# The opening of a layered kernel reordered: V projection by rows of Wv, two centred first tiles, evacuation per token tile

## The chip, the cores and the metric

The kernel runs on one core of one Trainium2 chip. The metric is device time in microseconds (us), the median of repeated executions. On one core the runs of one kernel mostly agree within 0.1%. Profiles are single executions taken by the hardware profiler; their spans are about 2 us shorter than the run times. Engines are named PE (matmuls), ACT (ScalarE), DVE (VectorE), POOL and SP. In the profiles PEld is PE's weight load, and an SPq line is the time SP spends on issuing a DMA, not the time until its data land. SP computes nothing; here it issues all DMAs, one after the other. PSUM is the memory that PE writes its sums to; an evacuation copies them out of it.

## The reference

```
x = A_x                                          # 2048 tokens x 1024, bf16
x = x + A(layernorm(x))                          # attention in a dilated window of 8, 32 heads of 32
x = x + B(layernorm(x))                          # token-mixing MLP 2048 -> 3584 -> 2048, gelu
x = x + A(layernorm(x))                          # the same weights again
x = x + B(layernorm(x))
# A: qkv = x @ wqkv (1024 x 3072); ...; o @ wo
```

The change concerns only the start of the first A: layernorm of the 16 token tiles (128 tokens each) and V = layernorm(x) @ Wv. Right after it the products for q and k begin, with weights of their own.

## The kernel before

`start_up` builds one list of steps for each engine. Each list is strictly kept in order. For each token tile k: statistics (`S_`, `A_`) on DVE, 1/std (`R_`: an Ln and an Exp) on ACT, the normalisation (`N_`) on DVE, and a transposed copy in `hT`, which is the matmul's stationary operand. Tiles 0 to 4 are transposed on PE (`tr`) and copied out of PSUM by ACT (`C_`); tiles 5 to 15 by a transposing DMA (`T_`). Then 16 matmuls (`V_`) and the evacuation of their sums (`E_`, ACT).

```python
wm = m_tile()
for _ in range(14):                               # warm-up matmuls on zeros
    chain_("PE", lambda: nc.tensor.matmul(wm[:], lhsT=warm[:, 0:P], rhs=warm[:], start=True, stop=True))
...
act = [(R_, 0), (C_, 0, 0), (R_, 1), (C_, 0, 1), (C_, 1, 0), (C_, 1, 1), (R_, 2), (E_, 0, 0), ...
       (R_, 5), (E_, 1, 1), (R_, 6), (E_, 2, 1), (C_, 4, 0), (C_, 4, 1)]
es = [(E_, k, n) for k in range(3, NT) for n in range(NDC)]   # NT = 16, NDC = 2 halves of a tile
rs = [(R_, k) for k in range(7, NT)]
for j, e in enumerate(es):
    act.append(e)
    if rs and j % 4 != 3:                         # three rsqrts per four half-tile evacuations
        act.append(rs.pop(0))
...
dve.append((zero_fill,))                          # after the last norm
dve.append((cast_biases,))
sp = [(T_, k) for k in range(np_, NT)] + [(load_biases,)]     # np_ = 5
...
# in the layer loop
start_up(v, wv)
wts = [None, None]
chain_("SP", load_qk, 0, wts)                     # weights of the first q and k, last on SP
...
for part, n in chunks:                            # part 0 is q, part 1 is k
    in_order(qk_chunk, 0, wts, part, n)           # first q matmuls, L352
```

The weights of q and k are issued on SP after every transposing DMA and after the biases, and the transposing DMAs wait for the norms, which wait for the rsqrts on ACT.

The softmax here doesn't subtract the row's maximum and nothing guards it: scores larger than these inputs give would overflow.

## Time and profile before

| | before |
|---|---|
| median of 6 runs | 1294.20 us (1293.59 to 1294.54) |
| span of the profiled run | 1291.8 us |
| first V matmul starts | 7.80 us |
| last norm ends, last transposing DMA issued | about 42.1 us |
| weights of q and k issued | 47.43 us |
| first q matmul (L352) starts | 65.62 us |

The first lines below are from the profile page (busy us, share of the span, number of instructions; then the chain that ended last, by engine).

```profile
PE 1275.1 (99%) x8286; PEld 593.4 (46%) x8442; DVE 417.1 (32%) x852; ACT 372.8 (29%) x628; POOL 2.4 (0%) x15
...
PE 98%; issue 1%; DVE 0%; ACT 0%
```

PE is the bound, and only time in which it stands idle, or runs slowly, can be won or lost. Next, PE's timeline in the opening: start, duration in us, engine, line, operation, output and inputs, number of matmuls merged, and in brackets the idle time before and what ended it.

```profile
1.38 5.30 PE L268 MATMUL m<-warm 128*128 128x512 bf16 x14 [1.38 <-DVE warm L207]
6.52 0.61 PE L244 MATMUL s<-ident,x 128*128 128x128 bf16 x8
7.80 1.04 PE L255 MATMUL m<-wv,hT 128*128 128x512 bf16 x4 [0.68 <-ACT hT L249]
8.81 0.62 PE L244 MATMUL s<-ident,x 128*128 128x128 bf16 x8
9.40 1.89 PE L255 MATMUL m<-wv,hT 128*128 128x512 bf16 x8
11.61 0.62 PE L244 MATMUL s<-ident,x 128*128 128x128 bf16 x8 [0.32 <-DVE x L188]
```

From the transposes at 6.52 on PE loses only about 1.5 us, in small gaps until 12.28 (an estimate: 59.1 us pass until q begins, and 256 matmuls at 0.216 us with five groups of transposes at 0.45 need 57.5). The last group is the same kernel's timeline (all engines) where the norms of the tiles end, and where q begins.

```profile
41.26 0.20 ACT L175 ACTIVATE rs<-ln 128x1 f32<-128x1 f32 x1
41.50 0.55 DVE L188 TENSOR_SCALAR x<-x,mv,rs 128x1024 bf16<-128x1024 bf16 x1 [0.60 <-ACT rs L175]
...
43.36 0.58 SPq L141 DMA_DIRECT2D b_bf<-in_B_b_dram  x1
...
44.00 3.39 SPq L142 DMA_DIRECT2D b_bf<-in_B_b_dram  x1
...
47.43 1.21 SPq L344 DMA_DIRECT2D wqk<-in_A_wqkv_dram  x2
...
65.62 7.07 PE L352 MATMUL m<-hT,wqk 128*128 128x512 bf16 x32
```

The weights were issued at 47.43 and landed 5.4 us later (median of the two loads), some 13 us before PE asked for them.

### The profile page before, as it was taken

What the parts mean: (1) busy time and instruction counts of PE and PEld (TensorE: products, weight loads), DVE (VectorE), ACT (ScalarE), POOL (GpSimd) and SP (SyncE); (2) the same over time, 40 slices, a digit from 0 to 9 for tenths busy, and PEclk for the clock granted to TensorE, in tenths of its full rate; (3) what the DMA queues carried; (4) which work ended last, traced back from release to release, by engine and by line L of the source; (5) the groups of instructions that cost most, each with busy time, mean ns of one, the idle gap of its engine ahead of it and who ended that gap; (6) DMA issues with size and microseconds to landing.
All of it is one profiled execution on the core that took longest, in us unless ns stands there. A gap on an engine that the chain in (4) does not pass through costs nothing.

```text
span 1291.8 us, 19417 instructions
## 1 busy us (share of the span) xinstructions
PE 1275.1 (99%) x8286; PEld 593.4 (46%) x8442; DVE 417.1 (32%) x852; ACT 372.8 (29%) x628; POOL 2.4 (0%) x15
## 2 busy tenths in 40 slices
PE   9999999999999999999999999999999999999999
PEld 4444444444444444444444444444444444444444
DVE  7457777820000022322300667778100000111111
ACT  5456664431111110000023666644311111000000
POOL 0000000000000000000000000000000000000000
PEclk9999999999999999999999999999999999999999
DMA  8411123742222235466410111247423222334330
GB/s 236 82 46 47 51 82 120 212 139 82 65 82 76 57 110 139 131 154 142 130 33 1 47 50 51 79 151 214 120 65 89 75 60 81 103 106 136 117 92 33
DMA packets 201862, 125.54 MB, mean 97 GB/s; under 512 B 39984, under 2 KB 183600, under 8 KB 201776
## 3 DMA queue, kind: packets, MB, share of 16 engines
q1 hardware_dynamic: 201776, 124.30, 34.2%
q8 instruction: 66, 1.08, 0.4%
q14 instruction: 20, 0.16, 0.0%
HBM read 96.48 MB, written 16.78 MB: 88 GB/s over the span
## 4 chain that ended last, share of the span: by engine, by line
PE 98%; issue 1%; DVE 0%; ACT 0%
PE m L352 17%; PE s L594 15%; PE s L547 15%; PE m L467 8%; PE acc L547 7%; PE m L547 7%; PE acc L594 7%; PE m L594 7%; PE m L337 4%; PE m L255 4%; PE s L383 2%; PE acc L418 1%; PE acc L422 1%; PE m L268 0%; PE s L244 0%
## 5 line engine op out<-in xcount | busy, mean ns | idle before, releaser
L594 PEld LDWEIGHTS <-w 128*128 128x128 bf16 x1820 | 177.0, 98 | 210.2
L547 PEld LDWEIGHTS <-w 128*128 128x128 bf16 x1792 | 175.3, 98 | 211.4
L352 PE MATMUL m<-hT,wqk 128*128 128x512 bf16 x963 | 223.3, 379 | 6.2 <-issue 4.6
L547 PE MATMUL s<-h,w 128*128 128x512 bf16 x878 | 201.2, 379 | 0.8
L594 PE MATMUL s<-g,w 128*128 128x512 bf16 (+1 forms) x912 | 201.0, 374 | 0.7
L596 DVE SCALAR_TENSOR_TENSOR xo<-s,b_sb,xs 128x512 bf16<-128x512 f32 (+1 forms) x33 | 24.4, 739 | 532.9 <-PE s L594 530.8
L352 PEld LDWEIGHTS <-wqk 128*128 128x128 bf16 x1024 | 95.3, 98 | 117.9 <-issue 10.7
L398 DVE TENSOR_TENSOR Pm<-pc,band 32x640 bf16<-32x640 bf16 x256 | 123.5, 483 | 56.3 <-ACT pc L386 49.4
L467 PE MATMUL m<-wo,oT 128*128 128x512 bf16 x500 | 110.6, 379 | 0.8 <-issue 0.3
L547 PE MATMUL acc<-h,w 128*128 128x512 bf16 x440 | 103.1, 379 | 0.5
L594 PE MATMUL acc<-g,w 128*128 128x512 bf16 x436 | 99.7, 379 | 0.5
L547 PE MATMUL m<-h,w 128*128 128x512 bf16 x438 | 98.5, 379 | 0.5
L594 PE MATMUL m<-g,w 128*128 128x512 bf16 (+1 forms) x436 | 96.9, 376 | 0.6
L174 ACT ACTIVATE ln<-mv,eps 128x1 f32<-128x1 f32 x64 | 18.9, 295 | 221.1 <-DVE mv L182 184.9
L467 PEld LDWEIGHTS <-oT 128*128 128x128 bf16 x512 | 49.6, 98 | 60.3 <-issue 1.3
L554 ACT ACTIVATE g<-s,b_sb 128x1024 bf16<-128x1024 f32 x28 | 31.2, 1114 | 158.2 <-PE s L547 146.4
L363 DVE COPY qB<-qs 32x512 bf16<-32x512 bf16 x136 | 38.1, 280 | 99.2 <-ACT qs L359 97.1
L255 PE MATMUL m<-wv,hT 128*128 128x512 bf16 x250 | 55.6, 379 | 1.0 <-ACT hT L249 0.7
L337 PE MATMUL m<-wv,hT 128*128 128x512 bf16 x251 | 55.2, 379 | 0.3
L386 ACT ACTIVATE pc<-s,shift 128x640 bf16<-128x640 f32 x64 | 51.2, 800 | 11.7 <-PE s L383 11.7
L359 ACT CAST qs<-m 128x512 bf16<-128x512 f32 x64 | 37.5, 586 | 48.7 <-PE m L352 47.6
L356 ACT CAST kT<-m 128x512 bf16<-128x512 f32 x64 | 37.5, 586 | 46.4 <-PE m L352 46.4
(58 smaller groups left out, 671.8 us busy)
## 6 DMA issues: line engine op xcount, KB each, us to landing
w<-in_B_w_dram SPq DMA_DIRECT2D x56, 512.0 KB, 3.8
w<-in_B_w_dram SPq DMA_DIRECT2D x64, 448.0 KB, 4.7
wqk<-in_A_wqkv_dram SPq DMA_DIRECT2D x16, 512.0 KB, 5.2
xa<-xn SPq DMA_DIRECT2D x32, 256.0 KB, 2.3
xs<-xa SPq DMA_DIRECT2D x32, 256.0 KB, 3.0
wv<-in_A_wqkv_dram SPq DMA_DIRECT2D x8, 512.0 KB, 5.6
wo<-in_A_wo_dram SPq DMA_DIRECT2D x8, 512.0 KB, 6.4
xr<-in_A_x_dram SPq DMA_DIRECT2D x16, 256.0 KB, 3.4
```

Of the source, the lines that this page charges most:

```text
L255: r = nc.tensor.matmul(pss_[k, n][:], lhsT=hT[:, kt, cols(*order[k])], rhs=wv[n][kt // 4][:, kt % 4, :], start=(kt == 0), stop=(kt == KD - 1))
L337: nc.tensor.matmul(ps[:], lhsT=hT[:, kt, cols(c, i)], rhs=wv[n][kt // 4][:, kt % 4, :], start=(kt == 0), stop=(kt == KD - 1))
L352: mm = nc.tensor.matmul(ps[:], lhsT=wts[part][:, kt, (g % 2) * P:(g % 2 + 1) * P], rhs=hT[:, kt, lo:lo + 512], start=(kt == 0), stop=(kt = ...
L356: nc.scalar.copy(out=kT[u % 2][:, ls], in_=ps[:])
L359: nc.scalar.copy(out=qs[:], in_=ps[:])
L363: nc.vector.tensor_copy(out=qB[u % 2][hp, h, ls], in_=qs[hp, :])
L386: nc.scalar.activation(out=pc[:].rearrange("p (n t) h k -> p n (t h k)", n=2), in_=ss[:, :, 0:2 * HG * GW], func=ACT.Exp, scale=scale, bia ...
L398: mm = nc.vector.tensor_tensor(out=Pm[rp, :, s0:s0 + HB, r * KG:r * KG + GW].rearrange("p h t k -> p t h k"), in0=pc[rp], in1=mk, op=ALU.mult)
L467: mm = nc.tensor.matmul(ps[:], lhsT=oT[g][:, cols(c, i)], rhs=wo[n][g // 4][:, g % 4, :], start=(g == 0), stop=(g == NG - 1))
L547: nc.tensor.matmul(pairs[fl][0][dc], lhsT=wt[c][:, i, fl * P:(fl + 1) * P], rhs=h2[c][i][:, dc * 512:(dc + 1) * 512], start=(k == 0), stop ...
L554: nc.scalar.activation(out=g[fb][:, fl, :].rearrange("p (n d) -> p n d", n=2), in_=t[:], func=ACT.Gelu_apprx_tanh, bias=b1_sb[:, ft:ft + 1])
L594: nc.tensor.matmul(ap, lhsT=w2t[ft // HF][:, ft % HF, c::DIL], rhs=g[ft // GF][:, ft % GF, lo:lo + w], start=(ft == 0), stop=(ft == FT - 1))
```

## The change

Its intent is to start the V product sooner. It has five parts:

1. Tiles 0 and 1 are only centred before their transposes (`M_` on DVE, half of tile 0 on ACT by `Ma`). 1/std is applied when V leaves PSUM. Their `hT` must be rewritten for q and k, so two norms are added on DVE (after those of tiles 8 and 9) and two transposing DMAs at the end of SP's list of transposes.
2. Wv is loaded by rows (all 1024 columns of one block of 128 rows, eight loads), and tiles 0 and 1 take turns row by row.
3. Sums lie in two-bank tiles, three in rotation; transposes move to the small PSUM tiles.
4. One evacuation per token tile (128x1024), not two halves.
5. The rsqrts are placed anew on ACT: one after each evacuation. Warm-up matmuls: 9, plus one after the first transposes, in place of 14. ACT's table load moves into `start_up`.

The core of the diff (cut: the new helper functions, the dependency table, the layout of Wv in the second layer):

```diff
-        for _ in range(14):
-            chain_("PE", lambda: nc.tensor.matmul(wm[:], ...))
+        for _ in range(9):
+            chain_("PE", W_, 1)
...
+        pe = [(tr, 0), (W_, 1), *VV(0, 0), (tr, 1), *VV(0, 1, 2), *VV(1, 0, 1, 2)]
...
+        act = [(Ma, 0, halves[1]), (C_, 0, 0), (C_, 0, 1), (C_, 1, 0), (C_, 1, 1), (R_, 0), (R_, 1), (R_, 2), (C_, 2, 0), (C_, 2, 1),
+               (R_, 3), (E_, 0), (E_, 1), (C_, 3, 0), (C_, 3, 1), (R_, 4), (E_, 2), (C_, 4, 0), (C_, 4, 1), (R_, 5), (E_, 3), (R_, 6)]
+        for k in range(4, NT):
+            act.append((E_, k))
+            if k + 3 < NT:
+                act.append((R_, k + 3))
-        for j, e in enumerate(es):
-            act.append(e)
-            if rs and j % 4 != 3:
-                act.append(rs.pop(0))
...
+            if k in (8, 9):
+                dve.append((N_, k - 8, whole))
-        sp = [(T_, k) for k in range(np_, NT)] + [(load_biases,)]
+        sp = [(T_, k) for k in (*range(np_, NT), 0, 1)] + [(load_biases,)]
```

More of the change, by code (lines that the diff above doesn't have):

```diff
@@ L113, in ln_exp_table @@
         return tc.keep_in_program_order(nc.scalar.preload_act_table_set("natural_log_exp_and_others"))
-    ln_exp_table()
     ident = const.tile([P, P], BF16, name="ident")
@@ L133 @@
                                 pattern=[[-1, GW]], channel_multiplier=1)
+    mv01 = const.tile([P, 2, 2], FP32, name="mv01")
+    rs01 = const.tile([P, 2], FP32, name="rs01")
+    nm0 = const.tile([P, 1], FP32, name="nm0")
     b1_bf = const.tile([P, FT], BF16, name="b1_bf")
@@ L187, in norm_dve @@
     def norm_dve(dst, x, mean, rs):
-        return nc.vector.tensor_scalar(out=dst, in0=x, scalar1=mean, scalar2=rs[:], op0=ALU.subtract, op1=ALU.mult)
+        return nc.vector.tensor_scalar(out=dst, in0=x, scalar1=mean, scalar2=rs, op0=ALU.subtract, op1=ALU.mult)
     def norm_act(dst, x, mean, rs):
@@ L205, in start_up @@
         np_ = 5
+        xc = [x2(f"xc{k}") for k in range(2)]
         warm = x2("warm", [P, 512])
@@ L217, in x_load, with w_load @@
             return r
-        def w_load(n, hf):
-            return nc.sync.dma_start(out=wv[n][hf][:], in_=wq_v[:, hf * (KD // 2):(hf + 1) * (KD // 2),
-                                                                2 * D + n * 512:2 * D + (n + 1) * 512])
+        def w_load(kt):
+            return nc.sync.dma_start(out=wv[kt // 2][:, kt % 2, :], in_=wq_v[:, kt, 2 * D:3 * D])
         def S_(k, cc):
@@ L228, in A_, with B_, M_, Ma @@
         def A_(k):
-            mvs[k] = st("mv", [P, 2])
-            return nc.vector.bn_aggr(out=mvs[k][:], in_=sts[k][:])
+            mvs[k] = mv01[:, k, :] if k < 2 else st("mv", [P, 2])[:]
+            return nc.vector.bn_aggr(out=mvs[k], in_=sts[k][:])
+        def B_(k):
+            return nc.vector.tensor_scalar(out=nm0[:], in0=mvs[k][:, 0:1], scalar1=-1.0, scalar2=None, op0=ALU.mult)
+        def M_(k, h):
+            return nc.vector.tensor_scalar(out=xc[k][:, h], in0=xs[k][:, h], scalar1=mvs[k][:, 0:1], scalar2=None,
+                                           op0=ALU.subtract)
+        def Ma(k, h):
+            return nc.scalar.activation(out=xc[k][:, h], in_=xs[k][:, h], func=ACT.Identity, bias=nm0[:])
         def R_(k):
-            rss[k] = st("rs", [P, 1])
-            return rsqrt(rss[k][:], mvs[k][:, 1:2], 1.0, eps1)
+            rss[k] = rs01[:, k:k + 1] if k < 2 else st("rs", [P, 1])[:]
+            return rsqrt(rss[k], mvs[k][:, 1:2], 1.0, eps1)
         def N_(k, hs):
@@ L241, in tr @@
         def tr(k):
-            tps[k] = pss.tile([P, KD, P], BF16, name="s", tag="s")
+            tps[k] = psm.tile([P, KD, P], BF16, name="m", tag="m")
             for kt in range(KD):
-                r = nc.tensor.transpose(tps[k][:, kt, :], xs[k][:, kt * P:(kt + 1) * P], ident[:])
+                r = nc.tensor.transpose(tps[k][:, kt, :], (xc[k] if k < 2 else xs[k])[:, kt * P:(kt + 1) * P], ident[:])
             return r
@@ L251, in V_, with E_ @@
         def V_(k, n, kts):
-            if kts[0] == 0:
-                pss_[k, n] = m_tile()
+            if k not in pss_:
+                pss_[k] = a_tile() if k % 3 == 1 else s_tile()
             for kt in kts:
-                r = nc.tensor.matmul(pss_[k, n][:], lhsT=hT[:, kt, cols(*order[k])], rhs=wv[n][kt // 4][:, kt % 4, :],
+                r = nc.tensor.matmul(pss_[k][:, n, :], lhsT=hT[:, kt, cols(*order[k])], rhs=wv[kt // 2][:, kt % 2, n * 512:(n + 1) * 512],
                                      start=(kt == 0), stop=(kt == KD - 1))
             return r
-        def E_(k, n):
+        def E_(k):
             c, i = order[k]
-            return nc.scalar.copy(out=v[c][i][:, n * 512:(n + 1) * 512], in_=pss_[k, n][:])
+            dst, src = v[c][i][:].rearrange("p (n d) -> p n d", n=NDC), pss_[k][:]
+            if k < 2:
+                return nc.scalar.activation(out=dst, in_=src, func=ACT.Identity, scale=rss[k])
+            return nc.scalar.copy(out=dst, in_=src)
         def T_(k):
@@ L266, in start_up, with W_ @@
         wm = m_tile()
-        for _ in range(14):
-            chain_("PE", lambda: nc.tensor.matmul(wm[:], lhsT=warm[:, 0:P], rhs=warm[:], start=True, stop=True))
+        def W_(n):
+            for _ in range(n):
+                r = nc.tensor.matmul(wm[:], lhsT=warm[:, 0:P], rhs=warm[:], start=True, stop=True)
+            return r
+        for _ in range(9):
+            chain_("PE", W_, 1)
         halves = (slice(0, D // 2), slice(D // 2, D))
         whole = (slice(0, D),)
+        chain_("ACT", ln_exp_table)
@@ L272, in start_up @@
         chain_("SP", x_load, 0, halves)
         chain_("SP", x_load, 1)
-        chain_("SP", w_load, 0, 0)
+        for kt in range(4):
+            chain_("SP", w_load, kt)
         chain_("SP", x_load, 2)
-        chain_("SP", w_load, 0, 1)
+        chain_("SP", w_load, 4)
+        chain_("SP", w_load, 5)
         chain_("SP", x_load, 3)
-        chain_("SP", w_load, 1, 0)
-        chain_("SP", w_load, 1, 1)
+        chain_("SP", w_load, 6)
+        chain_("SP", w_load, 7)
         for k in range(4, NT):
@@ L281, in start_up, with VV @@
             chain_("SP", x_load, k)
-        lo4, hi4 = range(KD // 2), range(KD // 2, KD)
+        def VV(k, *kts):
+            return [(V_, k, n, [kt]) for kt in kts for n in range(NDC)]
         a8 = range(KD)
-        pe = [(tr, 0), (V_, 0, 0, lo4), (tr, 1), (V_, 0, 0, hi4), (V_, 1, 0, lo4), (tr, 2), (V_, 1, 0, hi4),
-              (V_, 2, 0, a8), (V_, 0, 1, a8), (tr, 3), (V_, 1, 1, a8), (V_, 2, 1, a8), (tr, 4)]
+        pe = [(tr, 0), (W_, 1), *VV(0, 0), (tr, 1), *VV(0, 1, 2), *VV(1, 0, 1, 2)]
@@ L287, in start_up @@
+        for kt in range(3, 6):
+            pe += [*VV(0, kt), *VV(1, kt)]
+        pe += [(tr, 2), *VV(0, 6, 7), *VV(1, 6, 7), (V_, 2, 0, a8), (tr, 3), (V_, 2, 1, a8), (tr, 4)]
         pe += [(V_, k, n, a8) for k in range(3, NT) for n in range(NDC)]
-        act = [(R_, 0), (C_, 0, 0), (R_, 1), (C_, 0, 1), (C_, 1, 0), (C_, 1, 1), (R_, 2), (E_, 0, 0), (C_, 2, 0), (C_, 2, 1),
-               (E_, 1, 0), (R_, 3), (E_, 2, 0), (R_, 4), (E_, 0, 1), (C_, 3, 0), (C_, 3, 1), (R_, 5), (E_, 1, 1), (R_, 6),
-               (E_, 2, 1), (C_, 4, 0), (C_, 4, 1)]
@@ L291, in start_up @@
-        es = [(E_, k, n) for k in range(3, NT) for n in range(NDC)]
-        rs = [(R_, k) for k in range(7, NT)]
-        for j, e in enumerate(es):
-            act.append(e)
-            if rs and j % 4 != 3:
-                act.append(rs.pop(0))
-        dve = [(S_, 0, 0), (S_, 0, 1), (A_, 0), (S_, 1, 0), (N_, 0, halves), (S_, 1, 1), (A_, 1), (N_, 1, whole),
+        act = [(Ma, 0, halves[1]), (C_, 0, 0), (C_, 0, 1), (C_, 1, 0), (C_, 1, 1), (R_, 0), (R_, 1), (R_, 2), (C_, 2, 0), (C_, 2, 1),
+               (R_, 3), (E_, 0), (E_, 1), (C_, 3, 0), (C_, 3, 1), (R_, 4), (E_, 2), (C_, 4, 0), (C_, 4, 1), (R_, 5), (E_, 3), (R_, 6)]
@@ L298, in start_up @@
+        for k in range(4, NT):
+            act.append((E_, k))
+            if k + 3 < NT:
+                act.append((R_, k + 3))
+        dve = [(S_, 0, 0), (S_, 0, 1), (A_, 0), (B_, 0), (M_, 0, halves[0]), (S_, 1, 0), (S_, 1, 1), (A_, 1), (M_, 1, whole[0]),
                (S_, 2, 0), (S_, 2, 1), (A_, 2)]
@@ L300, in start_up @@
             nx = k + 1 < NT
-            if nx:
-                dve.append((S_, k + 1, 0))
-            dve.append((N_, k, whole))
+            if k == 2:
+                dve += [(N_, k, whole), (S_, k + 1, 0)]
+            else:
+                if nx:
+                    dve.append((S_, k + 1, 0))
+                dve.append((N_, k, whole))
             if nx:
                 dve += [(S_, k + 1, 1), (A_, k + 1)]
+            if k in (8, 9):
+                dve.append((N_, k - 8, whole))
         dve.append((zero_fill,))
         dve.append((cast_biases,))
-        sp = [(T_, k) for k in range(np_, NT)] + [(load_biases,)]
+        sp = [(T_, k) for k in (*range(np_, NT), 0, 1)] + [(load_biases,)]
         qs = {"PE": pe, "ACT": act, "DVE": dve, "SP": sp}
-        need = {cast_biases: lambda: (load_biases,) in done, R_: lambda k: k in mvs, N_: lambda k, h: k in rss, tr: lambda k: (N_, k) in done, C_: lambda k, hf: k in tps,
-                V_: lambda k, n, kts: ((C_, k, 1 if kts[-1] == KD - 1 else 0) in done or (T_, k) in done), E_: lambda k, n: (V_, k, n) in done,
-                T_: lambda k: (N_, k) in done}
+        need = {cast_biases: lambda: (load_biases,) in done, R_: lambda k: k in mvs, N_: lambda k, h: k in rss, tr: lambda k: (N_, k) in done if k > 1 else (M_, k) in done and (k == 1 or (Ma, k) in done),
+                B_: lambda k: k in mvs, M_: lambda k, h: k in mvs, Ma: lambda k, h: (B_, k) in done, C_: lambda k, hf: k in tps,
+                V_: lambda k, n, kts: ((C_, k, kts[-1] * 2 // KD) in done or (T_, k) in done), E_: lambda k: (V_, k, 1) in done and (k > 1 or k in rss),
+                T_: lambda k: (N_, k) in done and (k > 1 or (E_, k) in done)}
         done = set()
@@ L325, in load_wv, with fill_wv @@
     def load_wv():
-        return [[wt_("wv", [P, KD // 2, 512]) for _ in range(2)] for _ in range(NDC)]
-    def fill_wv(wv, n):
-        for hf in range(2):
-            nc.sync.dma_start(out=wv[n][hf][:],
-                              in_=wq_v[:, hf * (KD // 2):(hf + 1) * (KD // 2), 2 * D + n * 512:2 * D + (n + 1) * 512])
+        return [wt_("wv", [P, 2, D]) for _ in range(KD // 2)]
+    def fill_wv(wv):
+        for j in range(KD // 2):
+            nc.sync.dma_start(out=wv[j][:], in_=wq_v[:, 2 * j:2 * j + 2, 2 * D:3 * D])
     def v_proj(v, c, i, wv, ns):
@@ L336, in v_proj @@
             for kt in range(KD):
-                nc.tensor.matmul(ps[:], lhsT=hT[:, kt, cols(c, i)], rhs=wv[n][kt // 4][:, kt % 4, :],
+                nc.tensor.matmul(ps[:], lhsT=hT[:, kt, cols(c, i)], rhs=wv[kt // 2][:, kt % 2, n * 512:(n + 1) * 512],
                                  start=(kt == 0), stop=(kt == KD - 1))
@@ L603, in gemm2 @@
             mean, rs = stats(xo, 1.0, eps1)
-            norm_dve(xs[:], xo[:], mean, rs)
+            norm_dve(xs[:], xo[:], mean, rs[:])
             nc.sync.dma_start_transpose(out=hT[:, :, cols(c, i)], in_=xs[:])
@@ L619 @@
         else:
-            fill_wv(wv, 0)
-            fill_wv(wv, 1)
+            fill_wv(wv)
             wts = [None, None]
```

## The prediction

> **What bounds the kernel.** PE is busy 99% of a 1291.8 us span (busy table); the chain that ended last is 98% PE. Only idle PE time can be won. In the opening (timeline, chain of waits, 0 to 66 us) warm-up matmuls run 1.38 to 6.68, transposes start at 6.52, the first V matmul at 7.80 (after the rsqrt, the normalisation, 8 transposes and a copy), with gaps until 12.28. From there V runs at 0.216 us a matmul; the first q matmul (L352) starts at 65.62. V plus transposes need about 57.5 us, so the opening holds about 1.5 us of gaps after 6.5, and the lead before.
>
> **What the change does at the front.** Tiles 0 and 1 are only centred before the transposes; 1/std is applied at the evacuation. That takes Ln 0.29 + Exp 0.20 off the path, but adds a negated mean (a 128x1 DVE operation of this kind takes 0.205 us, group of L493) and puts half of the centring on ACT (estimate 0.7 us, from the 128x512 Gelu's 0.68). Mean is ready at 4.75; I expect ACT's half done at 5.7, transposes done near 6.25, first V matmul near 6.9 (0.9 earlier) (rows of Wv land in time, by the bytes moved per stretch plus the 1.1 us lag that x1 and x4 show). One new stall: R4 sits behind the copies of tile 3 on ACT, so transpose 4 waits about 0.7 us. Net at the front: V ends 0.3 to 1.1 us earlier, about 65.0.
>
> **What it moves at the back.** The order of instructions shows more. Before, ACT's rsqrts ran ahead (three per four half-tile evacuations), so the last norm ended near 42, the last transposing DMA issued at 42.1, biases at 43.4 and 44.0 (issue 3.39 us), wqk at 47.4, landing 5.4 us later at 52.8. Now ACT alternates strictly: whole-tile evacuation k, then rsqrt k+3. Evacuation k waits for V of tile k, so rsqrt 15 follows the evacuation of tile 12. Counting from the start s of V tile 13 on PE: evacuation to s+1.3 (1.11 us as the 128x1024 Gelu), rsqrt to s+1.86, norm (0.55) to s+2.45, last DMA transpose issued s+2.5. Two more transposing DMAs (tiles 0 and 1, 1.24 us of SP each) now stand before the biases. Before, from that issue to the landing of q's weights took 10.7 us; so now s+2.5+10.7+2.5 = s+15.7. V ends at s+10.35. PE therefore waits some 5.3 us for q's weights, however early V started. Earlier transposes still land 1.3 us before PE needs them. DVE's zero fill moves to about 57-64.5.
>
> The Trainium skill ("TensorE: Matmul & The Clock Gate", Part 1) says the PE clock halves after an idle window of about 3.4 us, free-running. The trace agrees with the cold start (warm-up matmuls 0.43 us apart until 5.6, then 0.22). A 5.3 us hole may hold such a window; then 4 us at half rate, +2 us. I count +1.
>
> **Sum:** -0.65 + 5.3 + 1 = +5.6 us: 1299.8 us, range 1297.0 to 1302.4. Faster by over 2%: 0.003; within 2%: 0.985; slower: 0.012. Layer 2 (its Wv lands long before) and everything later should not change.
>
> **Signs.** Right if: first V matmul near 6.9; last DMA transposes around 57 to 61 us; wqk issued near 65; PE idle about 5 us before the first q matmul, released by DMA wqk at about 70; matmuls 0.43 apart after it if the clock fell.
>
> **Wrong if:** wqk lands earlier (biases cheaper): the result is then 1293.5 to 1297; or transposes land late and every V tile stalls: over 1303.

## The result

| | before | after |
|---|---|---|
| median of 6 runs | 1294.20 us (1293.59 to 1294.54) | 1297.93 us (1295.78 to 1298.00) |
| span of the profiled run | 1291.8 us | 1296.0 us |
| first V matmul | 7.80 us | 7.03 us |
| last norm ends | 42.1 us | 56.8 us |
| weights of q issued | 47.43 us | 63.51 us |
| first q matmul | 65.62 us | 68.09 us |
| first score matmul | 72.62 us | 76.78 us |

The ratio after over before is 1.0027, with a 95% interval of 1.0014 to 1.0040. The change is slower by about 3.7 us, within 2%.

The front, PE's timeline of the changed kernel (the same view as before):

```profile
1.38 4.02 PE L285 MATMUL m<-warm 128*128 128x512 bf16 x9 [1.38 <-DVE warm L210]
5.25 1.10 PE L256 MATMUL m<-ident,xc 128*128 128x128 bf16 x8
6.14 0.63 PE L285 MATMUL m<-warm 128*128 128x512 bf16 x1
7.03 0.71 PE L267 MATMUL s<-wv,hT 128*128 128x512 bf16 x2 [0.25 <-ACT hT L261]
...
19.63 0.62 PE L256 MATMUL m<-ident,x 128*128 128x128 bf16 x8 [0.45 <-DVE x L190]
...
58.07 7.07 PE L267 MATMUL s<-wv,hT 128*128 128x512 bf16 x31
```

V starts 0.77 us sooner, but the transposes of tile 4 now wait 0.45 us for their norm (at 19.63). V matmuls then follow each other without a hole. The last line shows those of tiles 14 and 15 (32 matmuls; one record is missing). They end at 65.14, so the last one starts near 64.76, and without a wait q would have begun near 64.98, about 0.64 us sooner than before. That is the whole gain of the front.

The back, the timeline of the changed kernel around the end of V:

```profile
56.06 0.20 ACT L177 ACTIVATE rs<-ln 128x1 f32<-128x1 f32 x1
56.29 0.55 DVE L190 TENSOR_SCALAR x<-x,mv,rs 128x1024 bf16<-128x1024 bf16 x1 [2.06 <-ACT rs L177]
...
59.59 1.27 SPq L279 DMA_TRANSPOSE hT<-x  x1
...
60.91 0.57 SPq L143 DMA_DIRECT2D b_bf<-in_B_b_dram  x1
61.53 1.94 SPq L144 DMA_DIRECT2D b_bf<-in_B_b_dram  x1
...
63.51 1.20 SPq L374 DMA_DIRECT2D wqk<-in_A_wqkv_dram  x2
...
68.09 8.77 PE L382 MATMUL m<-hT,wqk 128*128 128x512 bf16 x32 [2.94 <-DMA wqk<-in_A_wqkv_dram]
```

Everything that ends SP's list sits 15 to 18 us later than before (the transposing DMA of tile 15 by 14.8, the biases by 17.5, the weights by 16.1), and PE stands idle 2.94 us until the weights of q land. The page still says PE 98% busy. Then comes a second loss: the 32 matmuls of the first q and k chunks took 8.77 us; before they took 7.07. The stretches of 2 us (columns: window, its length, busy time and instruction count of PE, PEld, DVE, ACT and POOL, then the granted PE clock, DMA share, GB/s) show why:

```profile
66.00:68.00 2.00, 0.00 (x0) 0.00 (x0) 0.35 (x2) 0.19 (x1) 0.00 (x0) 1.00 1.19 289
68.00:70.00 2.00, 1.91 (x6) 0.75 (x7) 0.00 (x0) 0.00 (x0) 0.00 (x0) 0.68 0.68 164
70.00:72.00 2.00, 2.00 (x6) 0.73 (x5) 0.25 (x1) 0.59 (x1) 0.00 (x0) 0.50 0.00 0
72.00:74.00 2.00, 2.00 (x10) 0.88 (x9) 0.89 (x4) 0.56 (x1) 0.00 (x0) 0.97 0.00 0
```

The clock was cut to half shortly after work had begun again. Finer stretches put the cut at 68.7 and the return at 72.1: 3.4 us at half rate, which costs 1.7 us. The two that hold the cut and the return:

```profile
68.60:68.80 0.20, 0.20 (x3) 0.07 (x2) 0.00 (x0) 0.00 (x0) 0.00 (x0) 0.81 1.19 289
72.00:72.20 0.20, 0.20 (x2) 0.04 (x1) 0.17 (x2) 0.00 (x0) 0.00 (x0) 0.66 0.00 0
```

The sum over the profiles closes: the first q matmul is 2.47 us late (65.62 to 68.09), the first score matmul 4.16 us late (72.62 to 76.78), and the whole span 4.2 us longer. Nothing of note after 77 us differs. Five of the six runs list a mean clock of 0.999 and took 1297.73 to 1298.00 us; the sixth kept 1.0 and took 1295.78. By that one run the clock drop is worth 2 us of the median; e3 below tests it.

### The profile page after: what moved, and what is told of

It is laid out like the page before. It is cut to its first block, busy times and chain, and to the rows that moved or that the text cites. A ratio compares the mean times of both kernels' runs of the same rounds, so it can differ in the third digit from the quotient of the medians.

```text
span 1296.0 us, 19405 instructions
## 1 busy us (share of the span) xinstructions
PE 1276.6 (98%) x8282; PEld 593.3 (46%) x8438; DVE 417.9 (32%) x854; ACT 370.7 (29%) x613; POOL 2.4 (0%) x15
## 4 chain that ended last, share of the span: by engine, by line
PE 98%; issue 1%; DMA 0%; DVE 0%; SPq 0%; ACT 0%
PE m L382 17%; PE s L624 15%; PE s L577 15%; PE m L497 8%; PE acc L577 7%; PE m L577 7%; PE acc L624 7%; PE m L624 7%; PE m L367 4%; PE s L267 2%; PE s L413 2%; PE acc L267 1%; PE acc L448 1%; PE acc L452 1%; DMA wqk<-in_A_wqkv_dram 0%
## 5 line engine op out<-in xcount | busy, mean ns | idle before, releaser
L367 PE MATMUL m<-wv,hT 128*128 128x512 bf16 x251 | 55.2, 379 | 0.3
L504 DVE TENSOR_TENSOR xn<-m,xr 128x512 bf16<-128x512 f32 x64 | 44.2, 691 | 16.9 <-PE m L497 16.4
```

What stands on the lines that cost most here:

```text
L367: nc.tensor.matmul(ps[:], lhsT=hT[:, kt, cols(c, i)], rhs=wv[kt // 2][:, kt % 2, n * 512:(n + 1) * 512], start=(kt == 0), stop=(kt == KD - 1))
L504: return nc.vector.tensor_tensor(out=xn[:, xs_], in0=pss_["o", n][:], in1=xr[:, xs_], op=ALU.add)
```

## The experiments

The theory: PE waits for q's weights because (a) the rsqrts are now paced by the evacuations, (b) SP issues the weights last, behind the transposing DMAs that wait for them, and (c) two more such DMAs stand before them; the hole then costs the clock. Rivals: the two added DMAs alone; the late zero fill on DVE; evacuation per tile, or the layout of Wv in layer 2; a clock loss of another cause. All kernels gave correct results. They were run in three groups (the first four, the next four, the last two), each on another chip and with its own runs of the kernel before: medians 1293.86, 1293.94 and 1293.77 us. So times of different groups are best compared by their distance to these. The diffs are cut to the lines that matter. They stand against the changed kernel for e1 to e4 and c1, against the kernel before for b1 and b2, and against c1, c2 and e3 for c2, d1 and d2.

| kernel | median us (range) | ratio to before, 95% interval | first q matmul | idle before it |
|---|---|---|---|---|
| e1_wqk_early | 1294.91 (1294.20 to 1295.11) | 1.0007 (0.9995 to 1.0020) | 65.99 | none |
| e2_rs_ahead | 1292.74 (1292.54 to 1293.16) | 0.9992 (0.9979 to 1.0004) | 64.58 | none |
| e3_fill | 1296.03 (1295.72 to 1296.10) | 1.0016 (1.0004 to 1.0029) | 67.92 | filled |
| e4_T01_early | 1293.74 (1293.28 to 1294.05) | 0.9999 (0.9985 to 1.0013) | 65.04 | 0.19 |
| b1_before_rs_paced | 1294.04 (1293.51 to 1294.17) | 1.0000 (0.9988 to 1.0013) | 66.24 | none |
| b2_before_paced_2T | 1298.36 (1296.99 to 1300.66) | 1.0034 (1.0020 to 1.0047) | 69.45 | 2.83 |
| c1_mended | 1292.40 (1292.29 to 1292.43) | 0.9988 (0.9976 to 1.0001) | 64.06 | none |
| c2_mended_no_centring | 1294.39 (1293.57 to 1295.44) | 1.0003 (0.9991 to 1.0016) | 66.31 | none |
| d1_no_centring_12warm | 1293.74 (1293.45 to 1294.16) | 1.0000 (0.9987 to 1.0012) | 65.17 | none |
| d2_fill4 | 1296.18 (1295.88 to 1297.79) | 1.0024 (1.0011 to 1.0038) | 67.61 | 2.11 |

### e1: the weights issued earlier

```diff
-        sp = [(T_, k) for k in (*range(np_, NT), 0, 1)] + [(load_biases,)]
+        sp = [(T_, k) for k in range(np_, 11)] + [(load_qk, 0, wts)] + [(T_, k) for k in (*range(11, NT), 0, 1)] + [(load_biases,)]
```

> The changed kernel with one thing moved: the load of the first q and k weights is issued in the middle of the transposing DMAs instead of after them and the biases. Theory (the loss is PE waiting for these weights, because their issue now comes last behind transposes paced by the evacuations, and the clock drop that this hole causes): first q matmul near 65.0, no hole, no clock drop, 1293.2 to 1293.8 us, a little under the kernel before. Rival (the late zero fill and bias casts on DVE, which stay late here, would stall q just as well): DVE copies of q late, 1295 or more. Rival (loss elsewhere, evacuation per tile or layer 2's layout of Wv): stays near 1297.9.

Measured 1294.91 us. The hole before q and the clock drop are gone, and the late zero fill (it still ended only at 65.6) held nothing up: the first copies of q on DVE started at 68.53. That rules out the zero fill, and per-tile evacuation and layer 2's layout, as causes of the loss. But the time missed the expected 1293.2 to 1293.8 because the move made a hole of its own. Of this kernel, PE's waits in the opening:

```profile
...
PE s L267 <- DMA hT<-x: 1.3, 1, 1.3
PE s L267 <- ACT hT L261: 0.5, 1, 0.5
PE m L256 <- DVE x L190: 0.4, 1, 0.4
```

The 1 MB of weights went ahead of the transposing DMA of tile 11, which then took 6.1 us to land where 3.1 is usual, and V of that tile waited 1.3 us. With the rsqrts paced by the evacuations, the transposes have little slack, and 1 MB of other traffic uses it up.

### e2: the rsqrts run ahead again

```diff
             act.append((E_, k))
-            if k + 3 < NT:
-                act.append((R_, k + 3))
+            for j in (2 * k - 1, 2 * k):
+                if j < NT:
+                    act.append((R_, j))
```

> The changed kernel with one thing moved: from tile 4 on, ACT computes two rsqrts after each evacuation instead of one, so they run ahead as in the kernel before. Theory (the pacing of the rsqrts is the root): last norm near 46, weights of q issued near 52 and landed by 58, no hole, no clock drop, 1293.2 to 1293.8 us. Rival (the two added transposing DMAs are what delays the weights): the hole stays, about 2.5 us, 1296 to 1298.

Measured 1292.74 us, a little better than expected. SP's timeline of this kernel:

```profile
43.41 5.98 SPq L279 DMA_TRANSPOSE hT<-x  x4
49.44 0.57 SPq L143 DMA_DIRECT2D b_bf<-in_B_b_dram  x1
50.07 1.93 SPq L144 DMA_DIRECT2D b_bf<-in_B_b_dram  x1
52.04 1.20 SPq L375 DMA_DIRECT2D wqk<-in_A_wqkv_dram  x2
```

And PE's, where q begins:

```profile
64.58 7.07 PE L383 MATMUL m<-hT,wqk 128*128 128x512 bf16 x32
```

The weights are issued at 52.04 with both added transposing DMAs still before them. So those two alone are not the cause, and moving one kind of step on ACT removes the whole loss. Every run of e2 was faster than every run of the kernel before in its group (1293.41 to 1294.13), though the interval of the ratio still touches 1.

### e3: the hole filled with dummy matmuls

```diff
+        pe.append((F_, 13))       # 13 matmuls on zeros into a fresh PSUM tile, after the last V
```

> The changed kernel with 13 matmuls of zeros (2.8 us of PE at full clock) after the last V matmul; the q weights are as late as ever. Tells the hole from the clock. Theory (about 2.9 us of waiting plus 1.7 to 2.1 us of half clock after it): first q matmul still near 68.1, no stretch at half clock, 1295.7 to 1296.2 us, as the one run of the changed kernel that kept its clock (1295.78). Rival (clock drop has another cause, or costs nothing): 1297.9 as before.

Measured 1296.03 us, as expected. PE's timeline:

```profile
64.83 2.97 PE L344 MATMUL m<-warm 128*128 128x512 bf16 x13
67.92 7.08 PE L391 MATMUL m<-hT,wqk 128*128 128x512 bf16 x32
```

Q starts at 67.92, nearly as late as in the changed kernel, but the 32 matmuls after it take 7.08 us and the clock stays at 1.0 in all five runs. So the loss splits into about 3 us of waiting and 1.6 to 1.9 us of clock (1297.93 less 1296.03 is 1.9; with each set against the kernel before of its own rounds, 3.73 less 2.17, it is 1.6).

### e4: the two added transposing DMAs earlier

```diff
-        sp = [(T_, k) for k in (*range(np_, NT), 0, 1)] + [(load_biases,)]
+        sp = [(T_, k) for k in (*range(np_, 12), 0, 1, *range(12, NT))] + [(load_biases,)]
```

> The changed kernel with the two added transposing DMAs (tiles 0 and 1) issued after that of tile 11, not after tile 15. Theory: rsqrts stay paced, but the q weights are issued 2.5 us earlier, land near 65.6, hole about 0.6 us, clock kept: 1293.8 to 1294.6 us. If the DMA engines rather than SP's issue set the time, the hole shrinks less: 1295 to 1297. Rival (the two DMAs cost nothing of the hole): 1297.9.

Measured 1293.74 us. The only wait of PE between 60 and 90 us:

```profile
PE m L382 <- DMA wqk<-in_A_wqkv_dram: 0.2, 1, 0.2
```

With the rsqrts still paced, taking 2.5 us of issue out of the last stretch is enough to make the hole almost vanish. It came out at 0.2 us, not the 0.6 expected. Neither part alone opens a hole of more than 0.2 us (e4, e2); both together open one of 2.94.

### b1 and b2: the loss rebuilt in the kernel before

b1 changes one line of the kernel before, so that its rsqrts are paced as in the changed kernel; b2 adds two repeated transposing DMAs (tiles 5 and 6, same data).

```diff
-            if rs and j % 4 != 3:
+            if rs and j >= 2 and j % 2 == 1:                     # b1 and b2
                 act.append(rs.pop(0))
...
-        sp = [(T_, k) for k in range(np_, NT)] + [(load_biases,)]
+        sp = [(T_, k) for k in (*range(np_, NT), np_, np_ + 1)] + [(load_biases,)]      # b2 only
```

> The kernel before with one thing changed: its rsqrts paced as in the changed kernel, one for tile k+3 after the second evacuation of tile k. No centring, no rows of Wv, no added transposes. Theory (pacing is the root): last norm near 57 instead of 42, q weights land between 66.0 and 68.0 (as the biases' issue costs 1.9 or 3.4 us), so a hole of 0.4 to 2.4 us before the first q matmul: 1294.3 to 1296.3 us, over 1297 only if the clock drops. Rival (the pacing is harmless without the rest of the change): 1293.9 as the kernel before.

> b1 with two transposing DMAs more before the biases (tiles 5 and 6 transposed a second time, same data). Theory: the whole loss of the changed kernel is rebuilt in the kernel before, without its front: hole 2.4 us longer than in b1, 2.9 to 4.8 us, clock drop in most runs: 1298.3 to 1301.0. Rival (the loss needs something else of the change): 1296 or less.

b1: 1294.04 us, the same as the kernel before. Here the rival as worded is right: pacing alone is harmless. The trace shows how narrowly. The weights were issued at 61.80 and the weight loads of PE's queue waited for them until 66.23, just when V's own matmuls ended: all the slack of the kernel before was eaten, and PE lost at most 0.2 us. b2: 1298.36 us. From PE's timeline:

```profile
69.45 8.43 PE L352 MATMUL m<-hT,wqk 128*128 128x512 bf16 x32 [2.83 <-DMA wqk<-in_A_wqkv_dram]
```

The hole is 2.8 us, a little under the 2.9 to 4.8 expected, and the clock fell in its trace too (at 68.8, while PE still stood idle), and by the mean clock in three of its five runs. So the loss of the change stands rebuilt without its front: no centring, no rows of Wv, no tile-wise evacuation. The spread of b2 (1296.99 with mean clock 1.0, 1300.66 with 0.997) comes with the clock.

### c1: both mended, and the wait of tile 4

e2 and e4 together, and `(R_, 4)` put before `(C_, 3, 0)` on ACT:

```diff
-               (R_, 3), (E_, 0), (E_, 1), (C_, 3, 0), (C_, 3, 1), (R_, 4), (E_, 2), ...
+               (R_, 3), (E_, 0), (E_, 1), (R_, 4), (C_, 3, 0), (C_, 3, 1), (E_, 2), ...
```

> The changed kernel with rsqrts run ahead (as e2), the two added transposing DMAs after that of tile 11 (as e4), and rsqrt 4 put before the copies of tile 3 on ACT. Theory: no hole; transposes of tile 4 no longer wait (0.45 to 0.6 us): first q matmul near 64.1, 1292.1 to 1292.4 us, about 1.6 under the kernel before. Rival (the wait of tile 4 is not gained, another follows): 1292.7 as e2.

Measured 1292.40 us, at the upper end of what was expected, 1.5 us under the kernel before of its group and 5.5 under the changed one (5.3 with each set against its own kernel before). Its five runs (1292.29 to 1292.43) lie below all nine of the kernel before in that group (1293.55 to 1293.99); the interval of the ratio, 0.9976 to 1.0001, does not quite exclude 1. The transposes of tile 4 start at 18.72 without a wait, and q starts at 64.06, 0.52 sooner than in e2. This is the best of the kernels run.

### c2 and d1: what the centring is worth

c2 is c1 without the centring and its two extra transposing DMAs; d1 is c2 with 12 warm-up matmuls in place of 9.

```diff
-        dve = [..., (A_, 0), (B_, 0), (M_, 0, halves[0]), (S_, 1, 0), (S_, 1, 1), (A_, 1), (M_, 1, whole[0]), ...
+        dve = [..., (A_, 0), (S_, 1, 0), (N_, 0, halves), (S_, 1, 1), (A_, 1), (N_, 1, whole), ...
-        act = [(Ma, 0, halves[1]), (C_, 0, 0), (C_, 0, 1), (C_, 1, 0), (C_, 1, 1), (R_, 0), (R_, 1), (R_, 2), ...
+        act = [(R_, 0), (C_, 0, 0), (R_, 1), (C_, 0, 1), (C_, 1, 0), (C_, 1, 1), (R_, 2), ...
-        for _ in range(9):
+        for _ in range(12):                                      # d1 only
```

> c1 without the centring: tiles 0 and 1 are normalised before their transposes as in the kernel before, no added transposing DMAs; rows of Wv, PSUM tiles and evacuation per tile stay. Tells what the centring itself gives at the front. Theory (it takes Ln, Exp and the order behind tile 1's statistics off the path): second transposes near 9.0 instead of 7.7, V ends 1.0 to 1.5 us later: 1293.2 to 1293.8 us. Rival (PE waits for rows of Wv anyway): same as c1 within 0.3.

> c2 with 12 warm-up matmuls in place of 9, because c2's trace shows the clock still cold at its first V matmuls (two in 1.04 us, four in 1.34 us) after PE had stood idle 0.9 us at 5.4. Theory (part of c2's loss was a late clock, not the missing centring): spread of the runs small again, 1293.2 to 1293.6 us, so the centring is worth 0.8 to 1.2 us of c1's gain. Rival (all of c2's loss is the missing centring): 1294.4 as c2.

c2: 1294.39 us, slower than expected and with a spread of 1.9 us. Its PE timeline at the front, and then that of d1:

```profile
6.29 1.03 PE L256 MATMUL m<-ident,x 128*128 128x128 bf16 x8 [0.88 <-DVE x L190]
7.11 0.63 PE L283 MATMUL m<-warm 128*128 128x512 bf16 x1
8.00 1.04 PE L267 MATMUL s<-wv,hT 128*128 128x512 bf16 x2 [0.25 <-ACT hT L261]
```

```profile
6.15 0.72 PE L256 MATMUL m<-ident,x 128*128 128x128 bf16 x8
6.70 0.38 PE L283 MATMUL m<-warm 128*128 128x512 bf16 x1
7.54 0.61 PE L267 MATMUL s<-wv,hT 128*128 128x512 bf16 x2 [0.46 <-ACT hT L261]
8.56 0.62 PE L256 MATMUL m<-ident,x 128*128 128x128 bf16 x8 [0.41 <-DVE x L190]
```

In c2 PE stood idle 0.88 us after its nine warm-up matmuls, and its first two V matmuls took 1.04 us, where d1's took 0.61: PE still ran at about half rate, as in its first matmuls. (The profile's granted clock reads 1.00 in both stretches, so this is read from the spacing alone.) So c2 mixed two effects, and d1 separates them. d1 took 1293.74 us (expected 1293.2 to 1293.6, just missed) with a spread of 0.7. Against c1, q starts 1.11 us later (65.17 to 64.06), and the medians differ by 1.3 us, from two groups of runs (1.5 by their distances to the kernel before). That is the worth of the centring in this order of steps; c1 with 12 warm-up matmuls was not run. In d1 these do not hold up the transposes: their weight load still waited for the norm on DVE until 6.14. And d1 equals the kernel before (ratio 1.0000): rows of Wv, the wider accumulators and the evacuation per tile gave nothing measurable without the centring.

### d2: a shorter hole

```diff
-        pe.append((F_, 13))
+        pe.append((F_, 4))
```

> e3 with 4 filling matmuls instead of 13, so that a hole of about 2.1 us is left before the q weights land near 68.1. Tells how long a hole may be. If the clock falls whenever PE is idle for most of one of the 3.4 us stretches that its drop and return show (68.7 to 72.1 in the changed kernel's trace), some runs fall and some do not: runs between 1296.0 and 1297.8. If only a hole near 3 us does it: all near 1296.0, as e3. If any hole does it: all near 1297.9.

Runs of 1295.88, 1296.10 and 1296.18 with mean clock 1.0, and 1297.70 and 1297.79 with 0.999. So a hole of about 2.1 us (2.11 in the profiled run, which kept its clock) still cost the clock in two of five runs, one of 2.94 in five of six, and a filled one (0.12 us of PE left idle between 66 and 68) in none of five.

## Why the prediction was right, and where it was off

- **The front** was right: first V near 6.9 (7.03 measured), a new wait at the transposes of tile 4 of about 0.7 (0.45 measured), V's end gained 0.65 us (0.64). The 0.45 us were real: c1 won 0.52 by moving one step.
- **The root** was right and is shown: the order on ACT delays the last norm from 42.1 to 56.8 us, which delays SP's queue, which delays q's weights. e2 undoes only the first link and the loss is gone. b2 rebuilds it in the kernel before. The start of V tile 13 was used as the origin of the sum; it came at 54.62, the last norm ended 2.2 us after it (2.45 predicted).
- **The weight of the two causes** was not put sharply. The prediction spoke of two transposing DMAs as 2.5 us of a 5.3 us hole, which leaves 2.8 us for the pacing. The runs show that pacing alone costs next to nothing (b1; a hole of 0.2 us in e4) and that the two DMAs alone cost nothing (e2): the first ate the slack, the second went past it.
- **The size of the hole** was off: 5.3 us predicted, 2.94 measured. The term that was mis-sized is the way from the issue of tile 15's transposing DMA to the landing of q's weights: 10.7 us as in the kernel before, plus 2.5 for the added DMAs. The profile has 11.2 us (56.87 to 68.04) in place of 13.2. The issue of the second bias load took 1.94 us and not 3.39, and the weights of q landed 4.5 us after their issue and not 5.4 (those of k 5.6); those two make 2.3 us. The remainder is the other way, the added DMAs taking 2.8 and not 2.5. The rest of the 2.4 us by which the hole was too long is that the chain began at 56.87 and not at s + 2.5 = 57.12, and that V ended at 65.14 and not at 64.97. Of the sooner start, 0.1 us is the evacuation: the Trainium skill ("ScalarE: Activation LUTs", "What ACT_TABLE_LOAD costs") says that each 128x1 pointer operand adds about 93 ns to an ACTIVATE; evacuations of 128x1024 with a scale of that kind took 1.10 us, plain ones 1.01. The prediction took 1.11 from a Gelu with a bias for a plain one. The trace of the kernel before was one sample: the same bias load took 1.9 to 2.3 us in the traces of e1 to e4, b1, b2, c1 and c2. Why it took 3.39 there stays open.
- **The clock** was counted at +1, as a chance of half for 2 us. It fell in five of six runs and cost 1.7 us in the trace, 1.6 to 1.9 by e3, 2.1 by the one run that kept it. The Trainium skill ("TensorE: Matmul & The Clock Gate", "Why this matters for your kernels") advises no idle gaps of PE over some 3 us between bursts; d2 shows that 2.1 can already do it.

So +5.6 was predicted and +3.7 measured: a hole 2.4 us too long, a clock drop 0.6 to 1.1 too cheap. The result of 1297.93 lies in the range (1297.0 to 1302.4), near its lower end, and that it lies there is partly luck. The prediction had named what would make it wrong: cheaper biases, so that the weights land earlier, and then 1293.5 to 1297. The biases were cheaper and the weights did land 2.3 us earlier than predicted (68.04, not 70.3); only the clock drop, counted at half, lifted the median back. The one run that kept its clock, 1295.78, lies in that other range. The chain of causes was right without luck; the total was not.

Could one have seen it without a run? Yes: the order of instructions gave it. The diff reads as a change of the front. What it cost happened 60 us later, through a list whose last entry is a load that nobody meant to move.

## What to carry to other kernels

When a change reorders one engine's queue, follow the queue to its end, and through every engine that waits for it: a step that runs ahead for free is slack for something issued last. Keep loads that a later stage needs out from behind a chain paced by the present stage, but mind where they go instead (e1 lost 1.3 us to that). When PE waits a few microseconds, count the clock too; here a wait of 2.9 us cost 1.6 to 2.1 more.

## What the Trainium skill lacked or had wrong

- "TensorE: Matmul & The Clock Gate", Part 1, gives the cold state after at least one idle window of about 3.4 us, free-running. Here PE was idle less than that and the clock fell 0.6 us after the matmuls had begun again (idle 65.1 to 68.1, half clock from 68.7 to 72.1). In b2 the 3.4 us before the fall at 68.8 even held about 1.2 us of busy PE. So, if the window ends at the fall, it need not be wholly idle. The page does not give the share that counts; the runs bound it only loosely (idle, by the profiled run of each, 1.3 us in e1: none of five runs fell; 2.1 in d2: two of five; 2.8 in b2: three of five; 2.9 in the changed kernel: five of six). That the half-rate stretch lasts 3.4 us agrees with the page's window.
- "DMA: Bandwidth & Descriptors", "DMA Transpose (X-bar)", lists constraints, and the page gives a bandwidth, but not how long one transpose takes from issue to landing, alone or beside other traffic. Here one of 128x1024 bf16 landed about 3.1 us after its issue (the median), and 6.1 us after when 1 MB of weights had been issued just before (e1).
- No page gives a time for what tiny scattered loads (the biases: 7 KB and 4 KB, in runs of 2 and 4 bytes) cost the issuing queue: 0.6 us and 1.9 to 3.4 us of SP in the traces here, in front of everything issued after them.
